# Relative-bias attention with a squared-ReLU layer: the bias table read back by another DMA queue

## The chip, the cores and the metric

The kernel runs on one core of a Trainium2 chip. The metric is the time of one execution on the device in microseconds (us); lower is better. The engines of a core are named as in the profile: PE (TensorE; PEld are its weight loads), DVE (VectorE), ACT (ScalarE), POOL (GpSimd) and SP (SyncE). Of these SP only issues DMAs here. POOL issues DMAs too, and those may convert from fp32 to fp16 on the way. ACT also issues a few at the start.

## The reference

```python
B, H, S, D = 8, 8, 576, 64            # batch, heads, sequence, head size
scores = (1 / sqrt(D)) * q @ k^T       # per batch and head, 576 x 576
n      = abs(i - j)
bucket = n if n < 16 else min(31, 16 + int(log(n / 16) / log(128 / 16) * 15))
scores = scores + bias_table[bucket]   # 32 buckets x 8 heads
attn   = exp(scores - max) ; attn = attn / (sum(attn) + 1e-9)
o      = attn @ v
x      = o with heads beside each other: 4608 rows x 512
h      = relu(x @ w_in)                # w_in 512 x 2048
out    = (h * h) @ w_out               # w_out 2048 x 512, out 4608 x 512 fp32
```

All inputs are fp32.

## The kernel before, in words

**Attention.** The scores are computed transposed, keys on the partitions. A unit of work is one batch `b`, a block `ic` of 192 query rows (three in 576) and a pair `hp` of heads: 96 units, listed in `UNITS`. For a unit PE computes the scores into the tile `st` (L615, L640), ACT takes their exponential into `et` (L666), DVE multiplies a band of `et` around the diagonal with the exponentials of the bias (`tb_sb`, L684, and a copy of it for the last 64 keys, `tm_sb`, L698). From distance 128 on the bias is constant and falls out in the normalisation, so only the band is multiplied. PE then multiplies with the values (`pv`, L774, L748), ACT and DVE normalise into `x_sb` (L816, L846, L827).

**The feed-forward part.** When all units of a block of rows are done, layer 1 (`hps`, L902) runs on it, ACT or DVE takes the ReLU (L913, L921), DVE squares it into `g_sb` (L917), and layer 2 (`yps`, L985) makes the output, which DVE scales (L998) and SP stores (L1001).

**The order.** No engine finds its order at run time. A planner (`Plan.run`) simulates the engines with fixed costs and due times, and the program is written out in that order. Each step is put with `add(engine, stream, occupied, latency, ...)`. Steps of one stream keep their order; among the streams of an engine the planner takes what can start first, or what is due first within a small window. `START` gives when each engine is free at first. A DMA that POOL issues (`pool(...)`) has a planned landing time worked out from a load; a DMA on SP has a fixed latency. The program order of each engine and each queue is therefore changed when any of these numbers is.

**The start.** The units of batch 0 come in the order of `FIRST`: head pairs 0 and 1 first, then 2 and 3. Before any unit can run, K and Q of its head pair have to be turned: PE does this by a matmul with an identity `id_sb` (L502), and DVE or ACT copies the result to `kt` and `qt` (L519, L517). The first K (heads 0 and 1) comes through SP as fp32 into `raw` (named `raw_k` in the profile) and is cast by DVE (L392); all others come through POOL into `kh` and `qh`. While no unit has reached its values, idle time of PE is filled with matmuls that compute nothing (`warm_up`, L367).

**The bias table.** ACT's queue loads the 32 x 8 table `bt_sb` and its last row `far_sb`. DVE subtracts (L400), ACT takes the exponential (`eb_sb`, L403), and PE multiplies it with the one-hot rows `oh_sb` (L409), which gives for each head one row of 512 values. DVE copies them to `tv_sb` (L414), SP writes that to the DRAM tensor `tdram` (named `t_bias`, 8 KB). It is then read back so that partition p gets the row shifted by p: `table_read`, three DMAs on POOL, for heads 0 and 1, 2 and 3, and 4 to 7, into `tb_sb`. The band multiplications of head pair `hp` wait for `tbs[hp]`.

All DMAs through these helpers are recorded at L251. In POOL's queue the loads around the table reads stand in this order: Q and K of pairs 0 to 2, V of heads 0 and 1 (four DMAs), the table reads for heads 0 to 3, V of heads 2 and 3, K and Q of pair 3 (`load_qk(0, 6, 2)`), the table read for heads 4 to 7, V of heads 4 to 7, then the weights `w_in` in four parts, with loads for batch 1 between them. POOL takes its DMAs in order: while one waits, the later ones are not issued.

Of the kernel before, what the change touches and what calls it, by code (L numbers as in the profile page):

```python
# [30 lines left out]
PT, TPP = 96, 6  # L31
# [9 lines left out]
F1_LAG, F2_LAG = 4.8, 19.5  # L41

NEXT = 4.0
START = {"POOL": 1.25, "DVE": 0.85, "PE": 1.25, "ACT": 2.9, "SP": 0.3}

MODE = 0.095
WAIT = {"ACT": 0.15, "DVE": 0.05}
# [44 lines left out]
class Plan:  # L92
# [10 lines left out]
    def add(self, eng, stream, occ, lat, fn, deps=(), due=0.0, load=0.0, rows=128, more=False):  # L103
        o = Op(eng, occ, lat, fn, deps, due, load, rows, more)
        self.streams.setdefault(eng, {}).setdefault(stream, deque()).append(o)
        return o
# [32 lines left out]
    def run(self):  # L139
        free = {**dict.fromkeys(self.streams, 0.0), **START}  # L140
        dma, rows, held = 0.0, 128, None
# [43 lines left out]
def kernel(  # L185
# [10 lines left out]
    nc = tc.nc  # L196
    assert (_bucket(np.arange(128, S)) == NBK - 1).all()

    def io(ins):
        return tc.keep_in_program_order(ins)  # L200
# [4 lines left out]
    oh_d = nc.inline_tensor(oh, name="c_oh")  # L205
# [3 lines left out]
    id_d = nc.inline_tensor(np.concatenate([eye, turned], axis=1), name="c_id")  # L209
    tdram = nc.dram_tensor("t_bias", (H, 512), FP16, kind="Internal")  # L210
# [14 lines left out]
    raw = single.tile([PT, 2, TPP * D], FP32, name="raw_k")  # L225
    id_sb = single.tile([PT, 2 * PT], FP16, name="id_sb")
    w_in_sb = single.tile([128, 4, 2048], FP16, name="w_in_sb")
    w_out_sb = single.tile([128, 16, 512], FP16, name="w_out_sb")
    tb_sb = single.tile([128, H, 384], FP16, name="tb_sb")
# [5 lines left out]
    oh_sb = single.tile([32, 512], FP16, name="oh_sb")  # L235
# [11 lines left out]
    add = plan.add  # L247


    def dma(eng, out_, in_):  # L250
        return lambda: io(eng.dma_start(out=out_, in_=in_))  # L251

    def pool(out_, in_, load, deps=(), occ=0.75):
        return add("POOL", "dma", occ, 0.0, dma(nc.gpsimd, out_, in_), deps, load=load)

    def load_qk(b, h0, n, which="kq"):

        return [
            pool(
                dst[:, h0 : h0 + n, :],  # L260
                src[b, h0 : h0 + n].rearrange("h (p t) d -> p h (t d)", t=TPP),
                0.6 * n,
            )
            for dst, src, name in zip(h16s[b][::-1], (k, q), "kq")
            if name in which
        ][::-1]

    def load_v(b, h, deps=()):

        vz = vzs[b % 2]  # L270
        e, o = h % 2, 64 * (h % 2)
        loads = [
            pool(
                vz[:, 0:4, h, o : o + 64],
                v[b, h, 0:512, :].rearrange("(t p) d -> p t d", p=128),
                1.02,
                deps,
            )
        ]
        if h < 2:  # L280
            loads.append(
                pool(
                    vz[o : o + 64, 4, e::2, o : o + 64],
                    v[b, e::2, 512:576, :].transpose([1, 0, 2]),
                    0.5,
                    deps,
                )
            )
        return loads
# [38 lines left out]
    small_in = []  # L328
    for out_, in_, t in (
        (bt_sb, bias_table, 3.2),  # L330
        (far_sb, bias_table[NBK - 1 : NBK, :].to_broadcast([NBK, H]), 3.6),
    ):
        dma(nc.scalar, out_, in_)()
        small_in.append(Op("ACT", 0.0, 0.0, None, []))
        small_in[-1].at, small_in[-1].done = 0.0, t
# [22 lines left out]
            )  # L358
        ]

    def small(out_, in_, lat):
        return add("SP", "set", 0.5, lat, dma(nc.sync, out_, in_))

    warm = psP.tile([128, 512], FP32, tag="p1", name="warm")

    def warm_up(n=4):
        io(nc.tensor.matmul(warm[:, 0 : 128 * n], km_sb[:, 0, :], km_sb[:, 0:n, :], start=True, stop=True))  # L367

    tvp = psP.tile([128, 512], FP32, tag="p0", name="tvp")
    k_raw = add(  # L370
        "SP", "set", 0.45, 3.4, dma(nc.sync, raw, k[0, 0:2].rearrange("h (p t) d -> p h (t d)", t=TPP))
    )
    small_in.append(small(oh_sb, oh_d.ap(), 2.8))
    id_in = small(id_sb, id_d.ap(), 2.8)
    loads_qk, loads_v = {}, {}
    loads_qk[0, 0] = [*load_qk(0, 0, 2, "q"), None]
    loads_qk[0, 2] = loads_qk[0, 3] = load_qk(0, 2, 2)
# [40 lines left out]
    written = add("SP", "set", 0.45, 3.5, dma(nc.sync, tdram.ap(), tv_sb), [tv])  # L418
    loads_v[0] = [x for h in range(2) for x in load_v(0, h, vz_set[0])]

    def table_read(h0, n):
        return pool(
            tb_sb[:, h0 : h0 + n, :],
            bass.AP(tensor=tdram, offset=512 * h0 + 1, ap=[[1, 128], [512, n], [1, 384]]),
            0.3 * n,
            [written],
        )

    def table_mixed(e):

# [9 lines left out]
            T0 + P * 7.5,  # L440
        )

    tbs = [table_read(0, 2), table_read(2, 2)]
    loads_v[0] += [x for h in range(2, 4) for x in load_v(0, h)]
    loads_qk[0, 6] = loads_qk[0, 7] = load_qk(0, 6, 2)
    tbs += [table_read(4, 4)] * 2
    loads_v[0] += [x for h in range(4, 8) for x in load_v(0, h)]
    tms = [table_mixed(e) for e in range(2)]
    w_ins, w_outs, halves, loads_v[1] = {}, {}, {}, []
# [640 lines left out]
```

## Time and profile before

| | |
|---|---|
| median of 8 runs | 425.99 us (424.85 to 427.92) |
| the profiled execution's own time | 424.85 us |
| its span in the profile | 423.1 us |
| PE busy | 408.5 us, 97% of the span |
| DVE busy | 314.1 us, 74% |
| ACT busy | 302.5 us, 71% |
| POOL busy (issuing DMAs, mostly) | 130.6 us, 31% |
| DMAs issued by POOL | 59.7% of 16 DMA engines |
| DMAs issued by SP | 17.1% of 16 DMA engines |

The span is what the profile covers; 1.75 us of the profiled execution's own time lie outside it. The shares are means over the whole span: at the start other engines are the busy ones than later. The granted clock is what the profile gives as the clock that PE was allowed, as a share of full speed. "Idle before" a row is the time the engine stood still ahead of it, and the arrow names what ended that.

### The profile page before, as it was taken

Reading aid. Unit: us, or ns where it says so; the run is one execution under the profiler, and the core shown is the slowest. Engines: PE = TensorE matmul, PEld = TensorE weight load, DVE = VectorE, ACT = ScalarE, POOL = GpSimd, SP = SyncE. Lnnn points to the kernel's source line nnn. Section 1 sums busy time; section 2 is a strip of 40 time slices with the busy share of each in tenths; the row PEclk is TensorE's granted clock in tenths of the full one; section 3 lists DMA queues with packets and bytes.
Section 4 is the critical chain, followed back from the end, with each engine's and each line's share of the span. In section 5 each row is a group of like instructions: output and inputs, shape, how many; then the busy total and the mean of one; then the engine's idle time right before and its main releaser. Section 6 shows DMA issues by size and latency. Waiting matters only on the chain.

```text
span 423.1 us, 9453 instructions
## 1 busy us (share of the span) xinstructions
PE 408.5 (97%) x3631; PEld 262.8 (62%) x3631; DVE 314.1 (74%) x940; ACT 302.5 (71%) x588; POOL 130.6 (31%) x176
## 2 busy tenths in 40 slices
PE   7979999999999999999999999999999999999996
PEld 4756786565675666666666666665666666665554
DVE  6777867578775777787778777787787877778762
ACT  5799879776897888778877878768877878771000
POOL 5966739505800193006800192006000000000000
PEclk8699999999999999999999999999999999999999
DMA  9999999949992599068973599158204200001012
GB/s 124 138 195 173 165 139 82 134 57 123 128 104 68 73 120 121 29 113 94 106 73 72 101 91 122 40 102 93 37 26 80 58 16 35 26 2 51 25 51 74
DMA packets 164765, 36.61 MB, mean 87 GB/s; under 512 B 152584, under 2 KB 160064, under 8 KB 164720
## 3 DMA queue, kind: packets, MB, share of 16 engines
q0 software_dynamic: 129728, 19.11, 59.7%
q1 hardware_dynamic: 34896, 16.90, 17.1%
q8 instruction: 28, 0.46, 0.5%
q14 instruction: 17, 0.14, 0.1%
q10 hardware_dynamic: 96, 0.00, 0.0%
HBM read 37.56 MB, written 16.52 MB: 128 GB/s over the span
## 4 chain that ended last, share of the span: by engine, by line
PE 83%; DVE 7%; ACT 6%; issue 1%; DMA 1%; DVEq 0%
PE yps L985 28%; PE hps L902 27%; PE pv L774 14%; PE st L640 7%; PE pv L748 4%; ACT et L666 3%; PE st L615 2%; DVE x_sb L827 2%; ACT r L816 1%; DVE et L684 1%; DVE rt L921 1%; DVE y L998 1%; DMA raw_k<-in_k_dram 1%; PE tp L502 1%; DVE kt L519 1%
## 5 line engine op out<-in xcount | busy, mean ns | idle before, releaser
L666 ACT ACTIVATE et<-st 128x960 f16<-128x960 f32 x192 | 167.9, 882 | 58.5 <-PE st L640 57.7
L902 PE MATMUL hps<-x_sb,w_in_sb 128*128 128x384 f16 (+1 forms) x896 | 150.9, 303 | 1.1 <-DVE rt L921 0.6
L985 PE MATMUL yps<-w_out_sb,g_sb 128*128 128x512 f16 (+1 forms) x592 | 148.5, 373 | 1.7 <-DVE y L998 1.5
L902 PEld LDWEIGHTS <-w_in_sb 128*128 128x128 f16 x896 | 83.0, 98 | 50.4 <-issue 3.3
L684 DVE TENSOR_TENSOR et<-et,tb_sb 128x384 f16<-128x384 f16 (+2 forms) x288 | 78.3, 311 | 34.5 <-ACT et L666 30.6
L251 POOL DMA_DIRECT2D vz<-in_v_dram x80 | 57.9, 752 | 131.9 <-PE pv L774 73.0
L985 PEld LDWEIGHTS <-g_sb 128*128 128x128 f16 x592 | 57.1, 98 | 48.9 <-issue 3.9
L827 DVE TENSOR_TENSOR x_sb<-pv,r 64x192 f16<-64x192 f32 x192 | 67.7, 353 | 24.1 <-ACT r L846 21.0
L774 PE MATMUL pv<-et,vz 128*128 128x192 f16 x804 | 84.5, 249 | 0.5 <-DVE x_sb L827 0.4
L917 DVE TENSOR_TENSOR g_sb<-rt 128x384 f16<-128x384 f16 x192 | 67.5, 355 | 8.0 <-ACT rt L913 4.1
L774 PEld LDWEIGHTS <-vz 128*128 128x128 f16 x804 | 62.6, 98 | 15.8 <-issue 13.5
L816 ACT ACTIVATE r<-pv 64x192 f32<-64x192 f32 x192 | 62.4, 325 | 8.2 <-PE pv L774 3.5
L913 ACT ACTIVATE rt<-hps 128x384 f16<-128x384 f32 x93 | 45.3, 487 | 25.4 <-PE hps L902 24.6
L921 DVE TENSOR_SCALAR rt<-hps 128x384 f16<-128x384 f32 x99 | 55.1, 557 | 10.5 <-PE hps L902 6.7
L640 PE MATMUL st<-qt,kt 64*128 64x192 f16 x768 | 51.3, 248 | 1.6 <-ACT et L666 1.6
L251 POOL DMA_DIRECT2D k<-in_k_dram x48 | 31.0, 692 | 26.4 <-DMA q<-in_q_dram 12.0
L846 ACT ACTIVATE r<-r 128x192 f32<-128x192 f32 x96 | 34.8, 363 | 3.0
L640 PEld LDWEIGHTS <-kt 64*128 64x128 f16 x768 | 32.0, 95 | 5.0 <-issue 3.2
L998 DVE TENSOR_SCALAR y<-yps 128x512 f32<-128x512 f32 (+1 forms) x37 | 24.9, 674 | 7.2 <-PE yps L985 6.5
L615 PEld LDWEIGHTS <-km_sb 128*128 128x128 f16 x192 | 18.4, 99 | 18.7 <-issue 3.7
L615 PE MATMUL st<-qt,km_sb 128*128 128x96 f16 x192 | 24.2, 208 | 1.4 <-ACT et L666 0.7
L251 POOL DMA_DIRECT2D q<-in_q_dram x18 | 24.6, 1416 | 0.0
(33 smaller groups left out, 117.4 us busy)
## 6 DMA issues: line engine op xcount, KB each, us to landing
out_dram<-y SPq DMA_DIRECT2D x35, 256.0 KB, 2.4
vz<-in_v_dram POOLq DMA_DIRECT2D x64, 64.0 KB, 3.2
q<-in_q_dram POOLq DMA_DIRECT2D x18, 192.0 KB, 7.9
k<-in_k_dram POOLq DMA_DIRECT2D x48, 72.0 KB, 7.2
w_in_sb<-in_moe_w_in_dram POOLq DMA_DIRECT2D x4, 512.0 KB, 8.9
w_out_sb<-in_moe_w_out_dram POOLq DMA_DIRECT2D x4, 512.0 KB, 11.0
qh<-in_q_dram POOLq DMA_DIRECT2D x8, 144.0 KB, 5.9
kh<-in_k_dram POOLq DMA_DIRECT2D x7, 144.0 KB, 6.3
```

What stands on the lines that cost most here:

```text
L251: return lambda: io(eng.dma_start(out=out_, in_=in_))
L615: nc.tensor.matmul(st[:, g, 2 * IC : 2 * IC + IC // 2], km_sb[:, p % KB, :], qts[p][:, ds(c0 + g * IC // 2, IC // 2)], start=True, stop=True,)
L640: nc.tensor.matmul(st[:, e, ds(i * IC, IC)], kts[p][rows, ts(2 * g + i, 128)], qts[p][rows, ds(c0, IC)], start=True, stop=True,)
L666: io(nc.scalar.activation(out=et, in_=sts[n, g][:, :, 0:w], func=EXPF, scale=SCALE))
L684: nc.vector.tensor_tensor(out=sl, in0=sl, in1=tb_sb[:, 2 * hp : 2 * hp + 2, ds(w0, w)], op=MULT)
L774: nc.tensor.matmul(pv if jt < 4 else pv.rearrange("p (g c) -> p g c", g=2), vz[:, jt, 2 * hp + e, :], ets[n, jt // 2][:, e, ds(jt % 2 * IC ...
L816: nc.scalar.activation(out=rs[n][o : o + 64, :], in_=pvt[n, e][64 - o : 128 - o, 0:IC], func=LNF)
L827: nc.vector.tensor_tensor(out=x_sb[o : o + 64, hp, ds(ring(blk), IC)][:, ::-1], in0=pvt[n, e][o : o + 64, 0:IC], in1=rs[n][o : o + 64, :], ...
L902: nc.tensor.matmul(hps[:, ds(i * w, w)], w_in_sb[:, kk, ts(nt, 128)], x_sb[:, kk, ds(o, w)], start=(kk == 0), stop=(kk == 3),)
L917: io(nc.vector.tensor_tensor(out=g_sb[:, ts(u, k), o : o + w], in0=rt, in1=rt, op=MULT))
L921: io(nc.vector.tensor_scalar_max(out=rt, in0=hpt[blks, u][:, 0 : 2 * IC], scalar1=0.0))
L985: nc.tensor.matmul(ypt[j], g_sb[:, nt, ds(128 * m % RING, 128)], w_out_sb[:, nt, cols], start=(nt == 0), stop=(nt == 15),)
```

## The change

The three table reads leave POOL's queue. In their place SP issues four, one for each head pair, straight behind its write of `t_bias`. The identity becomes the first DMA on SP's queue, ahead of `raw`. The one-hot rows move from SP's queue to ACT's, behind the two small table loads and ahead of the load of the activation functions. The planner's numbers follow: ACT is free at 3.3 instead of 2.9, `raw` has a latency of 3.3 instead of 3.4, the table reads 3.2, 4.2, 5.2 and 6.2.

```diff
-START = {"POOL": 1.25, "DVE": 0.85, "PE": 1.25, "ACT": 2.9, "SP": 0.3}
+START = {"POOL": 1.25, "DVE": 0.85, "PE": 1.25, "ACT": 3.3, "SP": 0.3}
...
     for out_, in_, t in (
         (bt_sb, bias_table, 3.2),
         (far_sb, bias_table[NBK - 1 : NBK, :].to_broadcast([NBK, H]), 3.6),
+        (oh_sb, oh_d.ap(), 4.5),
     ):
         dma(nc.scalar, out_, in_)()
...
-    def small(out_, in_, lat):
-        return add("SP", "set", 0.5, lat, dma(nc.sync, out_, in_))
-
...
+    id_in = add("SP", "set", 0.45, 2.8, dma(nc.sync, id_sb, id_d.ap()))
     k_raw = add(
-        "SP", "set", 0.45, 3.4, dma(nc.sync, raw, k[0, 0:2].rearrange("h (p t) d -> p h (t d)", t=TPP))
+        "SP", "set", 0.45, 3.3, dma(nc.sync, raw, k[0, 0:2].rearrange("h (p t) d -> p h (t d)", t=TPP))
     )
-    small_in.append(small(oh_sb, oh_d.ap(), 2.8))
-    id_in = small(id_sb, id_d.ap(), 2.8)
...
     written = add("SP", "set", 0.45, 3.5, dma(nc.sync, tdram.ap(), tv_sb), [tv])
     loads_v[0] = [x for h in range(2) for x in load_v(0, h, vz_set[0])]
 
-    def table_read(h0, n):
-        return pool(
-            tb_sb[:, h0 : h0 + n, :],
-            bass.AP(tensor=tdram, offset=512 * h0 + 1, ap=[[1, 128], [512, n], [1, 384]]),
-            0.3 * n,
-            [written],
-        )
+    def table_read(p):
+
+        rows = bass.AP(tensor=tdram, offset=1024 * p + 1, ap=[[1, 128], [512, 2], [1, 384]])
+        return add("SP", "set", 0.45, 3.2 + p, dma(nc.sync, tb_sb[:, 2 * p : 2 * p + 2, :], rows), [written])
+
+    tbs = [table_read(p) for p in range(4)]
...
-    tbs = [table_read(0, 2), table_read(2, 2)]
     loads_v[0] += [x for h in range(2, 4) for x in load_v(0, h)]
     loads_qk[0, 6] = loads_qk[0, 7] = load_qk(0, 6, 2)
-    tbs += [table_read(4, 4)] * 2
     loads_v[0] += [x for h in range(4, 8) for x in load_v(0, h)]
```

## The prediction

> **What bounds the kernel now.** I read the shares and slices of the page first, then the busy times by stage, then the chain that ended last, the waits of the first 30 us and the timeline of the start. The busy times by stage:
>
> ```profile
> 0.00:20.00 20.00, 17.16 (x183) 11.38 (x183) 13.46 (x44) 12.55 (x22) 15.23 (x26) 0.74 0.93 131
> 20.00:40.00 20.00, 15.58 (x198) 11.34 (x197) 15.92 (x53) 19.06 (x38) 12.89 (x20) 1.00 1.43 191
> 40.00:60.00 20.00, 19.05 (x264) 16.12 (x264) 15.57 (x48) 16.82 (x36) 12.18 (x15) 1.00 1.47 147
> ...
> 60.00:100.00 40.00, 38.83 (x353) 25.05 (x352) 28.36 (x87) 29.64 (x58) 18.41 (x24) 1.00 1.23 99
> 100.00:140.00 40.00, 38.97 (x375) 26.88 (x370) 29.15 (x93) 33.16 (x64) 16.35 (x21) 1.00 1.10 103
> 140.00:180.00 40.00, 39.86 (x340) 24.82 (x339) 29.34 (x92) 31.51 (x63) 15.58 (x20) 1.00 1.05 86
> ```
>
> The columns are the stretch, its length, then busy us of PE, PEld, DVE, ACT and POOL, the granted clock, DMA share and GB/s. From about 60 us on PE is full: it idles 1.2 and 1.0 us in the next two stretches and 0.14 in the one after. From 20 to 40 ACT is full (19.06 of 20) while PE idles 4.4 us. So the end is the sum of PE's work from 50 us on, and whatever PE or ACT loses before then is not made good later. The change lies in the first 20 us, so this start decides. Its lines:
>
> ```profile
> 0.74 0.39 SPq L251 DMA_DIRECT2D raw_k<-in_k_dram  x1
> ...
> 3.93 0.85 DVE L392 CAST kh<-raw_k 96x384 f16<-96x384 f32 x2
> ...
> 4.89 0.21 ACT L403 ACTIVATE eb_sb<-bt_sb 32x8 f16<-32x8 f32 x1 [1.94 <-DVE bt_sb L400]
> ...
> 5.27 0.45 PE L502 MATMUL tp<-id_sb,kh 96*64 96x96 f16 x12 [1.04 <-DMA id_sb<-c_id]
> ...
> 5.62 0.83 ACT L517 ACTIVATE kt<-tp 128x288 f16<-128x288 f32 x2 [0.53 <-PE tp L502]
> ...
> 6.76 0.31 SPq L251 DMA_DIRECT2D t_bias<-tv_sb  x1
> ...
> 8.25 3.49 ACT L666 ACTIVATE et<-st 128x960 f16<-128x960 f32 x4 [0.90 <-PE st L640]
> ...
> 11.02 1.45 POOL L251 DMA_DIRECT2D tb_sb<-t_bias  x2 [3.68 <-DMA t_bias<-tv_sb]
> ```
>
> PE waits 1.04 us for the identity, and the first exponential starts at 8.25. SP's write of the table goes out at 6.76, and POOL, which had finished its earlier issues at 7.33, stands still 3.68 us until that write has landed. Nothing behind it in POOL's queue is issued meanwhile. Then the first use of the table, and the turning of head pair 3 later:
>
> ```profile
> 14.73 2.71 DVE L684 TENSOR_TENSOR et<-et,tb_sb 128x384 f16<-128x384 f16 x12 [0.52 <-DMA tb_sb<-t_bias]
> ...
> 17.15 0.33 ACT L816 ACTIVATE r<-pv 64x192 f32<-64x192 f32 x1 [0.74 <-PE pv L774]
> ...
> 21.43 0.68 PE L502 MATMUL tp<-id_sb,qh 96*64 96x96 f16 x12 [0.52 <-DVE kt L519]
> ...
> 23.60 0.26 PE L615 MATMUL st<-qt,km_sb 128*128 128x96 f16 x2 [0.53 <-DVE qt L519]
> ...
> 24.17 0.97 ACT L666 ACTIVATE et<-st 128x960 f16<-128x960 f32 x1 [0.34 <-PE st L640]
> ```
>
> DVE waits only 0.52 us for the table itself. The last three lines are pair 3: its K and Q, issued behind the stall at 13.92 and 14.56, are turned in the stage in which ACT is full, and ACT then stands 0.34 us.
>
> **The identity first, the raw K second.** SP's issues take 0.39 to 0.42 us, 0.46 apart. The identity now goes out at 0.74 and lands between 2.9 us (the one-hot rows) and 3.6 us (its own row) later, at 3.6 to 4.3 instead of 5.27. The raw K goes out at 1.20 and, with its 3.17 us, lands at 4.4 instead of 3.91. The first of the two casts (0.43 us each) ends at about 4.85: there PE starts, 0.4 us earlier than 5.27. But the other steps behind the casts move by 0.45 the wrong way. On DVE casts, subtraction and table copy share one stream; the subtraction goes from 4.71 to 5.2 or 5.3, and the exponential of the table on ACT from 4.89 to about 5.4. If the planner keeps that exponential ahead of the first copy of K, that copy starts at 5.62 as now, and nothing is won. Bounds: -0.4 and 0; I take -0.2, since either engine may take the copies.
>
> **The one-hot rows on ACT's queue.** One issue more of about 0.44 us (its neighbours' rows) ahead of the table load (1.67, 1.28 us): ACT is ready at 3.4 instead of 2.95. It has idled 1.94 us before its first use at 4.89, so this costs nothing; without that cover it would cost the 0.44. The rows go out at about 1.65 and land 2.9 to 3.1 us later (one-hot and far rows), by 4.75; PE uses them at 5.64 now. Zero.
>
> **The table through SP.** The table copy of DVE (6.06) now follows memsets that end at 6.07, which swallow part of the 0.45, so the write goes out about 0.15 later, at 6.9. It was seen as landed 4.26 us after its issue (6.76 to 11.02), so by 11.15. SP issues the read of pair 0 and it lands after 3.2 us (raw K, 288 KB on SP with little beside it) to 4.3 us (SP's 256 KB stores between 60 and 100 us, beside busy POOL loads): 14.35 to 15.45, against 14.73. Pair 0 is the read that counts, since DVE waited for it; bounds -0.4 and +0.7. I take 0: the read has 192 KB, less than both rows, but POOL's loads now run beside it. Pair 1 issues 0.45 us later; DVE needs it after the first six of its twelve multiplications, some 1.3 us after pair 0. Pairs 2 and 3 landed at 20.7 (15.20 plus 5.5) and can only come earlier. Four issues of 0.3 to 0.45 us stand on SP behind the wait for the write; the next thing SP does is at 75.79, so nobody is behind them.
>
> **POOL set free.** Three issues leave it (1.45 and 0.83 us) and so does the wait of 3.68. V of heads 2 and 3 goes out at 7.33 instead of 12.44, K and Q of pair 3 at about 8.8 instead of 13.92, the first `w_in` part some 6 us earlier than 18.89. The DMA engines had work until about 10 us and then nothing until 12:
>
> ```profile
> 9.00:10.00 1.00, 0.88 (x12) 0.50 0.91 60
> 10.00:11.00 1.00, 1.00 (x18) 0.50 0.07 4
> 11.00:12.00 1.00, 1.00 (x22) 0.50 0.00 0
> 12.00:13.00 1.00, 1.00 (x15) 0.50 0.36 95
> ```
>
> (Here: PE busy, granted clock, DMA share, GB/s.) About 2.5 us of the hole are filled, so data come at least that much sooner. Worth: pair 3 can be turned between 14 and 18.6, where PE runs fillers and DVE idles (1.19 us before 18.64). Then ACT's copy of its Q (0.49 us at 22.25) leaves the full stage, and so do ACT's 0.34 of waiting and PE's 0.52 and 0.53. On ACT that is 0.83 us, on PE 1.05; ACT is the bound there, so I take -0.8. The weights come sooner, but PE's holes until 30 us have another reason (layer 1 needs the first rows, normalised at 29.8), and PE idles 1.28 us from 30 to 40, of which I count -0.4. Bounds: 0, if ACT's stage absorbs both, and -2.3, the 1.05 and all of the 1.28.
>
> The Trainium skill, page "DMA: Bandwidth & Descriptors", section "Issuing engines are not separate DMA queues", says that spreading DMAs over issuing engines saves only the time to issue, because all run on the same 16 engines. By that rule alone this term would be 0; the idle DMA engines between 10 and 12 us are what it leaves out, and no run here shows yet what filling them brings.
>
> **The clock.** PE was granted 0.50 from about 7.4 to 17.6 us, though its busy time is 1.00 in nearly each of these us. I count no shift of that. The page "TensorE: Matmul & The Clock Gate", Part 1, has the clock rise after some 3.4 us of sustained work; these rows, 7 us of busy PE at half clock, do not agree with it.
>
> **The order.** The planner writes another order for everything. After 60 us PE idles 2.95 us up to 400, so a new order can give back little there and I count 0, with 1 us either way in the range.
>
> **The sum.** -0.2 + 0 + 0 - 0.8 - 0.4 = -1.4 us: 423.45 for the profiled execution (424.85, the fastest of the eight, 1.14 below their median), and 425.99 - 1.4 = 424.6 for the median. About 0.3%, 1.3 us, is what a measurement of this kernel can tell from no change.
>
> **Rivals.** *The loads were covered anyway* (chance 0.30): ACT's stage from 20 to 50 is bound by its own work, an earlier pair 3 only changes which instruction waits, and 0 to -1 us is left: 425.5. For it: ACT was at 97% there. Against it: the three waits above name pair 3.
>
> *The table comes late* (slower, 0.25). POOL's loads keep the DMA engines busy where the table's write and reads found them empty (0.07 and 0.00 in the rows above). The write takes 4.26 plus up to 1 us, the first read 4.3: pair 0 at 16.45. DVE's order is fixed, so the multiplications, the first values and whatever copies are queued behind them on DVE move by 1.7; on ACT there was already 0.74 of waiting at 17.15. It decides if pair 0 lands after 16 us: below that the -1.2 of the freed POOL outweighs it. With the -1.2 gone, as the same copies wait, it gives +1.7: 427.7.
>
> *The change does not do what it says*: a read on SP could be held by something other than the write. SP is empty from 6.76 to 75.79, so I give this no share of its own.
>
> **Chances.** Forecast, faster: 0.45. Within 0.3%: 0.30. Slower: 0.25. The range goes from all gains with half a us from the order (-0.4 - 0.4 - 2.3 = -3.1, of which I keep -3.0: 423.0) to most of the late table (+1.5: 427.5).
>
> **What would show it.** The first turning matmul at about 4.85 with a wait for DVE's cast, not for the identity; the first exponential between 7.85 and 8.25; no wait of POOL for `t_bias`, and DMA shares near 1 between 10 and 12 us; DVE's first multiplication between 14.3 and 15.5; pair 3 turned before 19 us and ACT's busy time from 10 to 20 above its 7.73. I am wrong if the first multiplication comes after 16, if pair 3 comes sooner and the end doesn't, or if PE's idle time after 60 us grows by over 1 us.

## The result, and the profile after

The changed kernel takes 429.84 us (median of 11 runs, 428.30 to 431.63) against 426.07: ratio 1.0083, interval 1.0066 to 1.0101. It is slower by 3.8 us between the medians, where I had forecast 1.4 us faster. Its profiled execution took 431.63 with a span of 429.7, so it lies 1.8 us above its own median, as the one of before lay 1.2 below; single waits of these two profiles are to be read with that in mind.

The stages of the changed kernel, in the columns used before (stretch, length, busy us of PE, PEld, DVE, ACT and POOL, granted clock, DMA share, GB/s):

```profile
0.00:20.00 20.00, 17.52 (x188) 11.30 (x188) 14.65 (x47) 12.50 (x21) 16.00 (x27) 1.00 1.21 164
20.00:40.00 20.00, 16.48 (x209) 12.29 (x207) 16.24 (x53) 17.71 (x36) 12.25 (x19) 0.91 1.31 169
40.00:60.00 20.00, 18.11 (x247) 15.41 (x245) 15.95 (x50) 16.11 (x33) 10.55 (x13) 1.00 1.56 154
...
140.00:180.00 40.00, 36.99 (x306) 22.91 (x305) 27.06 (x82) 28.95 (x58) 15.58 (x20) 0.96 0.96 83
```

Up to 60 us PE is busy for 52.1 us against 51.8 before. By then it has done 14 matmuls of layer 1 fewer (144 against 158) and 9 of the attention more. At their mean times in these profiles (0.25 us for one of layer 1, 0.24 to 0.29 for the others) that is about 1 us of work less, by estimate. So the start, where every edit of the change lies, holds a small part of the loss at most. From 140 to 180 PE idles 3.0 us, where it idled 0.14. The whole stretch from 60 to 400 us in the same columns, first of before, then of the changed kernel:

```profile
60.00:400.00 340.00, 337.05 (x2879) 212.86 (x2877) 258.09 (x775) 253.54 (x493) 90.27 (x117) 1.00 0.73 76
60.00:400.00 340.00, 331.94 (x2847) 210.28 (x2846) 252.06 (x762) 254.41 (x496) 89.67 (x116) 0.99 0.70 74
```

PE idles 8.06 us there, where it idled 2.95. The start in lines of the timeline:

```profile
0.74 0.35 SPq L251 DMA_DIRECT2D id_sb<-c_id  x1
...
4.83 0.71 PE L496 MATMUL tp<-id_sb,kh 96*64 96x96 f16 x12
...
9.04 3.49 ACT L660 ACTIVATE et<-st 128x960 f16<-128x960 f32 x4 [1.73 <-PE st L634]
...
9.68 1.94 SPq L251 DMA_DIRECT2D tb_sb<-t_bias  x4
...
15.50 2.71 DVE L678 TENSOR_TENSOR et<-et,tb_sb 128x384 f16<-128x384 f16 x12 [0.50 <-DMA tb_sb<-t_bias]
...
21.71 0.45 PE L496 MATMUL tp<-id_sb,qh 96*64 96x96 f16 x12 [1.11 <-DVE kt L513]
```

The wait for the identity is gone, and POOL has no wait for the table any more. The first exponential is later (9.04 for 8.25), and so is the first use of the table (15.50 for 14.73). Pair 3 is still turned in the full stage: its K at 19.88 and its Q at 21.71, for 20.20 and 21.43 before.

Where the time went shows later, in the same timeline (start, busy us, engine, line, operation):

```profile
157.10 1.31 SPq L561 DMA_TRANSPOSE kt<-k  x1
...
165.31 0.46 DVE L548 COPY km_sb<-kt 64x64 f16<-64x64 f16 x2 [3.21 <-DMA kt<-k]
...
166.93 1.86 PE L979 MATMUL yps<-w_out_sb,g_sb 128*128 128x512 f16 x4 [3.01 <-DVE y L992]
```

SP turns K of head pair 16 by a DMA transpose issued at 157.10. It lands 8.2 us later. DVE's next step is the copy of that pair's last 64 keys into `km_sb`, which nobody needs until the next batch begins. DVE takes its steps in order, so it stands for 3.21 us; behind it stands the scaling of an output tile, and PE, waiting for that tile's bank, stands for 3.01. Behind this wait the granted clock is 0.50 from 167 to 170 us, and the four matmuls at 166.93 take 1.86 us, where four of the same took 1.03 at 155.82.

The transpose of this pair was slow in the profile of before too (6.0 us). But there DVE's copies came 9.0 us after its issue and waited for nothing:

```profile
153.09 1.20 SPq L567 DMA_TRANSPOSE kt<-k  x1
...
162.13 0.36 DVE L554 COPY km_sb<-kt 64x64 f16<-64x64 f16 x2
```

In the changed kernel DVE is ready for them 5.0 us after the issue (at 162.10, the 165.31 less the wait). The waits of this kind in all, from the list of waits after 60 us (sum, times, longest), first of before, then of the changed kernel:

```profile
DVE km_sb L554 <- DMA kt<-k: 1.4, 3, 0.6
```

```profile
DVE km_sb L548 <- DMA kt<-k: 6.8, 3, 3.2
...
PE yps L979 <- DVE y L992: 5.2, 5, 3.0
```

The three waits are for pairs 11, 16 and 22. Head pairs from 8 on are turned by SP (`turn`, L561), far from any line that the change edits. What has changed there is the order: the planner, given other times for POOL and the table, has written other programs for PE, ACT, DVE and SP nearly everywhere after the start.

### The profile page after: what moved, and what is told of

It is laid out like the page before. It is cut to its first block, busy times and chain, and to the rows that moved or that the text cites. A ratio compares the mean times of both kernels' runs of the same rounds, so it can differ in the third digit from the quotient of the medians.

```text
span 429.7 us, 9455 instructions
## 1 busy us (share of the span) xinstructions
PE 410.6 (96%) x3630; PEld 263.9 (61%) x3630; DVE 315.4 (73%) x943; ACT 301.2 (70%) x585; POOL 128.5 (30%) x173
## 4 chain that ended last, share of the span: by engine, by line
PE 75%; DVE 11%; DMA 7%; ACT 4%; issue 1%; SPq 0%; DVEq 0%
PE yps L979 26%; PE hps L896 25%; PE pv L768 14%; PE st L634 6%; DMA kt<-k 5%; PE pv L742 3%; DVE et L678 2%; ACT et L660 2%; PE st L609 2%; DVE x_sb L821 2%; DVE rt L915 2%; DMA tb_sb<-t_bias 1%; DVE y L992 1%; DVE g_sb L911 1%; ACT r L810 1%
## 5 line engine op out<-in xcount | busy, mean ns | idle before, releaser
L768 PE MATMUL pv<-et,vz 128*128 128x192 f16 x804 | 85.7, 249 | 3.4 <-DVE x_sb L821 1.9
```

Of the source, the lines that this page charges most:

```text
L768: nc.tensor.matmul(pv if jt < 4 else pv.rearrange("p (g c) -> p g c", g=2), vz[:, jt, 2 * hp + e, :], ets[n, jt // 2][:, e, ds(jt % 2 * IC ...
```

## Experiments

My theory after these lines was that the new order costs the time; the rival, that the moved DMAs do, by landing late themselves or by disturbing later ones. All ratios are to the kernel before, run beside the experiment.

**The moved DMAs in the old order, and the new order with the old DMAs.** In the first, the planner plans the kernel before, steps of POOL and SP that issue nothing keeping their planned place, and only the issuing is exchanged:

```diff
-    written = add("SP", "set", 0.45, 3.5, dma(nc.sync, tdram.ap(), tv_sb), [tv])
+    written = add("SP", "set", 0.45, 3.5, write_and_read, [tv])   # write, then four reads on SP
...
-        return pool(tb_sb[:, h0 : h0 + n, :], bass.AP(...), 0.3 * n, [written])
+        return add("POOL", "dma", 0.75, 0.0, lambda: None, [written], load=0.3 * n)
```

The identity, `raw` and one-hot DMAs are exchanged likewise. PE's, ACT's and DVE's instructions are the old ones one by one.

> All DMAs as in the changed kernel (table through SP, identity first, one-hot rows on ACT's queue), but PE, ACT, DVE and POOL keep the order of the kernel before. Order theory (the loss comes from the order that the planner wrote anew, not from the moved DMAs): within 1.5 us of before, 424.5 to 427, ratio 0.996 to 1.002. Traffic theory (the moved DMAs themselves disturb the start and later transfers): the loss of the change stays, 429 to 430.5, ratio about 1.008.

Measured: 425.94 us, ratio 1.0009 (0.9989 to 1.0030). The second is the reverse: the changed kernel's order, with the table reads on POOL at their old place in its queue and the start's DMAs on their old queues.

> The reverse: the order of the changed kernel on PE, ACT, DVE, and on POOL and SP, but the table read back by POOL at its old place and the start's DMAs on their old queues. Order theory: 429 to 431, ratio 1.006 to 1.011. Traffic theory: about 426, ratio within 0.003 of 1.

Measured: 429.60, ratio 1.0104 (1.0082 to 1.0126). So the loss comes with the order, and none that can be measured with the moved DMAs. The waits come with the order too: with the old DMAs DVE waited 5.1 us for `kt` after 60 us, most of it (1.4, 1.6 and 1.9 us) for the same three pairs 11, 16 and 22. The traffic theory, my rival of the late table, falls.

**The two parts of the moves, in the old order.** The table alone:

> Only the table moves to SP (four reads behind the write, POOL freed), and every engine keeps the order of the kernel before. My prediction gave the freed POOL -1.2 us and the table 0: 424.2 to 425.5 and a ratio of 0.996 to 1.000. If the table's later landing under POOL's traffic (4.9 to 8.0 us on SP in earlier runs, against 3.7 on POOL) costs more than the freed loads give: 426.5 to 428.

Measured: 426.05, ratio 1.0016 (1.0000 to 1.0031). The start's DMAs alone:

> Only the start moves (identity first, raw K second, one-hot rows on ACT's queue), in the order of the kernel before; the table stays with POOL. The prediction gave it -0.2 us. The run with the start alone and a planner's order that differed in a few early instructions was 0.5% slower; if that came from the moved DMAs: 427 to 428 here too; if from those few instructions: within 0.3% of before.

Measured: 426.10, ratio 1.0008 (0.9988 to 1.0028). Neither part gains anything that can be measured: the -1.2 us that I gave to the freed POOL is not there. With the order held, pair 3 is turned at its old place in PE's program, so what turning it earlier would bring was not tried. This result agrees with the rule of the Trainium skill, page "DMA: Bandwidth & Descriptors", section "Issuing engines are not separate DMA queues", which the prediction had set aside.

**The two parts, planned anew.** The table alone, with the planner free to reorder:

> Only the table moves to SP, with its planned latencies; the start's DMAs stay on their old queues and places. The planner writes a new order of everything (PE's, ACT's and DVE's programs differ from before nearly everywhere after the start). Order theory: a few us off before in either direction, since this order is again another one; if what is planned for POOL without the table reads is what makes the order bad, 428.5 to 431, ratio 1.006 to 1.012. If the loss needs the start's part: within 0.3% of before.

Measured: 432.43, ratio 1.0155 (1.0124 to 1.0187): above even the 428.5 to 431 that I gave for an order made bad by the freed POOL. The start alone:

> Only the start moves: identity first, raw K second, one-hot rows on ACT's queue; the table stays with POOL. The order changes in a few instructions of the first 10 us alone. Order theory: within 0.3% of before (424.6 to 427.2), with a first exponential up to 1 us later than 8.25. If the later first exponential were the cause of the loss: 427 to 428.

Measured: 427.14, ratio 1.0047 (1.0026 to 1.0068): the ratio is above the 0.3% of the order theory and so speaks for the later first exponential, which came at 9.39 in its profile. But that is not the cause: with all moved DMAs in the old order it came at 9.78, and the ratio was 1.0009. The order differs only in the first 10 us, by four fillers, one copy of K on DVE instead of ACT and the place of a few memsets. Yet the profile has five waits of DVE for K after 60 us, 4.6 us in all, against 1.4 in three before. These copies stand in the old order, so here it is not their place that changed but the time at which DVE and the transposes reach it. That this is the whole loss was not tried.

**The stalled copies.** A first test moved DVE's copies for every pair that SP turns, after the planning, by up to 8 us of the plan:

```diff
-    for o in plan.run():
-        o.fn()
+    order = plan.run()
+    for p in range(4 * DMA_FROM, 4 * B):
+        use = min(o.at for o in order if any(d in km_ready[p] for d in o.deps))
+        for c in km_ready[p]:
+            due = min(c.at + 8.0, use - 2.5)
+            ...                       # c goes ahead of the first step at or after due
+    for o in order:
+        o.fn()
```

> The changed kernel with one thing moved: DVE's copies into km_sb for the head pairs that SP turns stand later in DVE's program, by up to 8 us of the plan; all other engines keep their order. Copy theory (DVE waits for K that a slow DMA transpose brings late, with everything behind it, and PE runs dry): 3 to 5 us of the loss go, 425 to 427.5, ratio 0.998 to 1.003, and the profile shows no wait of DVE for kt. If the new order loses in many small places instead: 429 or more, ratio at least 1.006.

Measured: 427.77, ratio 1.0058 (1.0036 to 1.0081). The waits for `kt` fell to 0.4 us, but only part of the loss went, a little less than I expected. The same move in the kernel before:

> The same move of the copies in the kernel before. It had 1.4 us of such waits on DVE and PE nearly full through them. Copy theory: 0 to 1 us faster, 425 to 426.3, ratio 0.9975 to 1.0. If the place of these copies matters by itself (bank or buffer held longer): slower by over 1 us.

Measured: 427.74, ratio 1.0047 (1.0031 to 1.0064). This is the slower outcome: moving all copies has a price of its own, and the first test mixed a gain with a loss. The next moves only pair 16's two copies (`for p in (16,)` in the loop above), 19 steps back in DVE's program:

> The changed kernel with a single step moved: DVE's two copies of the last keys of head pair 16, on which DVE stood 3.2 us at 162 to 165 us of the profile, stand 19 instructions later in DVE's program. Copy theory: 1.5 to 3.5 us of the loss of 3.8 go, 426.5 to 428.3, ratio 1.002 to 1.006. If that event belongs to the profiled execution alone, or the wait only moves: 429 or more.

Measured: 427.43, ratio 1.0048 (1.0030 to 1.0065). Two copies of 0.2 us each in another place take away 0.35%, 1.5 us, of the changed kernel's 0.83%. Last, the copies of the three pairs that stalled (`for p in (11, 16, 22)`), six steps in all:

> The changed kernel with DVE's copies of the last keys moved later for the three head pairs that DVE waited for in its profile (11, 16 and 22; 1.6, 3.2 and 1.9 us). Copy theory for the whole loss: 1 to 2 us better than with pair 16 alone, 425.5 to 426.8, ratio 0.9995 to 1.003. If the rest of the loss lies in the order elsewhere: the same as with pair 16 alone, ratio 1.003 to 1.007.

Measured: 425.94, ratio 0.9991 (0.9970 to 1.0012). The whole loss is gone, and nothing else in the changed kernel's order was touched. PE's idle time from 60 to 400 us goes the same way: 8.06 us in the changed kernel, 5.27 with pair 16 moved, 3.62 with all three, 2.95 before. PE's busy time, granted clock, DMA share and GB/s in the three stretches of the stalls, in the changed kernel, with pair 16's copies moved, and with all three moved:

```profile
100.00:110.00 10.00, 8.79 (x73) 1.00 1.53 127
160.00:170.00 10.00, 6.99 (x52) 0.83 1.96 134
240.00:250.00 10.00, 9.19 (x82) 1.00 0.58 98
```

```profile
100.00:110.00 10.00, 8.76 (x71) 1.00 1.56 126
160.00:170.00 10.00, 9.87 (x84) 1.00 1.96 139
240.00:250.00 10.00, 10.00 (x85) 1.00 1.00 106
```

```profile
100.00:110.00 10.00, 10.00 (x88) 1.00 1.55 133
160.00:170.00 10.00, 9.87 (x83) 1.00 1.52 113
240.00:250.00 10.00, 9.64 (x77) 1.00 1.20 95
```

The move of pair 16 fills the second stretch and leaves the first as it was; the move of pair 11 fills the first. In the third the middle kernel shows less than there is: its wait for pair 22, 1.8 us, ends at 236.9, ahead of the stretch. DVE's waits for `kt` are 0.7 us in all then:

```profile
DVE km_sb L548 <- DMA kt<-k: 0.7, 2, 0.4
```

**The same cure for the moved DMAs in the old order.** That kernel had one long wait of this kind, 1.9 us for pair 18 (2.7 us in three waits).

> All moved DMAs with the order of the kernel before, and DVE's copies for head pair 18 later, for which it stood 1.9 us in that kernel's profile. If such a wait costs what it did for pair 16 (1.5 us of the end for 3.2 us of waiting): 0.5 to 1 us faster than without the move, 424.5 to 425.7, ratio 0.997 to 1.000. If the wait was that execution's alone: 1.000 to 1.002.

Measured: 426.12, ratio 0.9999 (0.9977 to 1.0020), not to be told from the 1.0009 without it. The longest wait for `kt` is 0.7 us in its profile, but the gain that I expected did not come: not every such wait reaches the end. So no version here is faster than the kernel before.

**The order as a draw.** Three kernels leave every DMA in its queue and change one number of the planner. Two of them change the planned load of a part of the weights from 3.1 to 3.3; first on the kernel before, then on the changed one:

> The kernel before with one number of the planner changed, the planned load of one part of the weights of layer 1 from 3.1 to 3.3. No DMA moves to another queue or place; only the order of PE, ACT, DVE and SP is written anew. If any new order costs or wins some us (the order is a draw, and the one before was a good one): off by 0.3 to 1%, more likely slower. If only the freed POOL makes bad orders: within 0.3%.

Measured: 428.89, ratio 1.0080 (1.0058 to 1.0103). DVE waited only 1.7 us for `kt` in its profile, so this order loses in another way, which stays open.

> The changed kernel with the same one number of the planner changed as in the run on the kernel before (the planned load of a part of the weights 3.1 to 3.3). No DMA moves. Draw theory: another order, another time: off from the changed kernel's 429.8 by over 1 us in either direction (426 to 433). If the freed POOL makes bad orders whatever the numbers: 429 to 431.

Measured: 430.23, ratio 1.0113 (1.0086 to 1.0141): slower than the changed kernel by 0.4 us by the medians, less than the 1 us that I expected, and in the range that I gave to a freed POOL making bad orders. That rival does not explain the run before it, where POOL is not freed and the order is bad all the same. The third lets the planner know of slower transposes:

> The changed kernel with the planned latency of SP's DMA transposes at 6.0 instead of 3.4, so that the planner itself puts DVE's copies and the scores later. Copy theory: the waits of DVE for kt shrink from 6.8 us to under 2 and 2 to 3.5 us of the loss go: 426.3 to 428. If the place of these copies is not the matter: 429.5 or more.

Measured: 433.09, ratio 1.0174 (1.0147 to 1.0201), where I had expected 429.5 or more if the place of the copies is not the matter. The waits for `kt` halved (one of 3.3 us stayed), but layer 1 now waited for DVE's ReLU (3.0 us in two waits). So this was no test of the copies alone: a planner's number moves hundreds or thousands of steps, and only a move made after planning separates one from the rest.

## Why the prediction was wrong

**The order: the step that failed.** I counted the new order at 0, with 1 us either way, because PE idled only 2.95 us after 60 us. That idle time bounds what a new order can win there. What it can lose is not bounded by it: a full engine has no slack, and one step in the wrong place makes it stand. PE's idle time from 60 to 400 us grew by 5.1 us, where I had named 1 us as a sign of being wrong. With the DMAs as before, the new order cost 1.04%; one changed number of the planner cost the kernel before 0.80%. Six orders written anew were all slower than the old one, by 0.5 to 1.7%. So the old order was a good one, by luck or by choice, which no run here tells; I held the schedule that I had seen for the schedule that the planner makes. Nor did the 1 us go into the range: its lower end is the sum of the gains, its upper end the late table, and neither holds a term for the order. The 0.25 that I gave to a slower kernel rested on the late table, too, and not on the order.

**The freed POOL, -1.2 us: fell.** K of pair 3 went out at 8.77 as reckoned (8.8), and the DMA share in the hole from 10 to 12 us rose to 1.16 and 1.00. But pair 3 was hardly turned earlier for it (19.88 and 21.71, for 20.20 and 21.43): its place in PE's program is the planner's. So the -0.8 us for turning it before 19 us never had its condition. The -0.4 us for the earlier weights had it, the first part going out at 12.98 instead of 18.89. In the old order the table's move, with the weights, measured +0.16% at its middle. That fits my rival, that the loads were covered anyway.

**The table, 0: the terms were both off.** The write landed after 2.6 us (7.11 to 9.68), not 4.26; the four reads on SP then took from 5.8 to 8.0 us each, in the answer on the tile `tb_sb`, where my upper bound was 4.3:

```profile
DMA to landing us min/median/max: 5.8/6.9/8.0
```

That bound was the median of three stores, of which one had taken 5.4. The two errors nearly cancel: 15.5 is just above the bound of 15.45. It cost nothing that could be measured, as the run with the old order shows.

**The start, -0.2: the mechanism right, the end not.** The first turning came at 4.83 (4.85 foretold), set by the cast; the identity had landed 1.7 us after its issue, sooner than the 2.9 to 3.6 reckoned. The close agreement is partly luck: in the other profiles with this start the turning came between 4.82 and 5.59. The later first exponential is not the change's: the kernel with one changed number of the planner has the start's DMAs and order of before, and began it at 9.12 in its profile. Its 12 turning matmuls took 0.69 us, as they took 0.71 here, and 0.45 in the profile of before. The start alone, in the old order, measured 1.0008.

**The sum.** -1.4 us is a ratio of 0.9967, below all that the moved DMAs measured in the old order (0.9989 to 1.0030). So the gains were too large, and the term for what the diff does to the planner, 0, was the one that decided.

## What to carry to other kernels

When a kernel's order is written by a planner, an edit of any input has two effects: what the edit does on the chip, and a new order. Hold the order and exchange the issue to see the first, hold the DMAs and take the new order to see the second, before any term of the edit is believed. Look for the steps on which an engine stands for a DMA while their result is not needed yet: three pairs of 0.2 us copies put too early were worth 0.9% here (1.0083 against 0.9991). Move only those: moving every such copy cost the kernel before 0.47%.

## What the runs showed of the hardware

Reads that SP issues beside POOL's loads land late: 4.5 to 8.0 us for 192 KB in the profiles with the table on SP, against 3.6 to 5.1 (3.7 in the profile of before) when POOL issued them while the DMA engines were nearly idle (a share of 0.01 to 0.10 from 10 to 12 us). SP's DMA transposes of 2.8 us at the median took 8.2 us where SP issued one at 157.10 and POOL was issuing its own DRAM to DRAM loads of Q and K from 152.12 on. For the same pair it was 6.0 us in the profile of before, and 6.9 to 8.7 us in seven others: with the new order and the old DMAs, with the table alone planned anew, and in the five kernels made from the changed one. That POOL's traffic is the cause was not tried by itself.

The clock column is 1.00 for the first 20 us of the changed kernel, but eight score matmuls took 0.82 us at 12.91, just as at 12.12 in the profile of before, where the column says 0.50; at 18.21 eight of them took 0.51. So the column missed a stretch of half clock at the start of this profile.
